# Chunk 0 of a Sinkhorn attention and feed-forward kernel: queries in both halves of the rows, sorted keys copied whole, and products of zeros in the head

## The chip, the cores and the metric

The kernel runs on one core of one Trainium2 chip. The metric is device time in microseconds (us) of one execution. A core has TensorE (PE: matrix products and transposes, results into PSUM), VectorE (DVE), ScalarE (ACT), GpSimd (POOL) and SyncE (SP), each with its own instruction queue that is worked off in order, and DMA engines that move data between the HBM and SBUF. The engines wait for each other by semaphores.

## The reference

Attention with sorted blocks, followed by a feed-forward stage. There are 4 batches of 8 heads, 768 positions of 64 elements, in 8 blocks of 96. A Sinkhorn loop turns each head's 8x8 matrix into a nearly doubly stochastic one; keys and values of a block become sums over all blocks with these weights; each block of queries then attends to its own sorted block.

```python
P = sort_net
for _ in range(5):
    P = np.exp(P - np.max(P, axis=-1, keepdims=True))
    P = P / (np.sum(P, axis=-1, keepdims=True) + 1e-09)
    P = P / (np.sum(P, axis=-2, keepdims=True) + 1e-09)
k_sorted = np.einsum('bhij,bhjcd->bhicd', P, k_b)
v_sorted = np.einsum('bhij,bhjcd->bhicd', P, v_b)
scores = scale * np.matmul(q_b, k_sorted.transpose(0, 1, 2, 4, 3))
attn = softmax(scores)
x = np.matmul(attn, v_sorted)        # (B*S, 512) after a transpose
h = x @ w_in                         # 512 -> 2048
out = (h * np.cos(h)) @ w_out        # 2048 -> 512
```

## The kernel before

The 3072 tokens go through in 8 chunks of 384: chunk n is four blocks (`IC` = 4) of one batch, all 8 heads. The order of instructions on each engine is the order of the program text (`tc.manual_schedule()`), so a helper that is called earlier stands earlier in every queue that it uses. Chunk n's feed-forward (`moe_up`, then `moe_down`) carries in its slots the attention of chunk n + 1. Chunk 0 has nothing to stand beside it: its attention is the head of the program.

The head runs so. The 8x8 matrices of two batches lie in one group of 128 rows, so there are two groups g. After a first normalization, four Sinkhorn rounds (the loop over `it`, lines 311 to 337) alternate between engines: ScalarE takes exponentials (line 313), TensorE sums columns by a product with the matrix `same` (`product`, line 252), VectorE takes reciprocals and forms the next matrix (lines 332 to 335). `spread` (line 273) writes a group's final weights into a block matrix `bds`. In rounds 1 and 2 `q_turn` (line 286) transposes the queries of chunk 0 on TensorE, sixteen pieces a call, and ScalarE copies them out of PSUM one round later.

With the weights, `v_turn` (line 405) lays out a second copy for the values. `k_sort_0` (line 349) makes the sorted keys of chunk 0: products of the loaded keys (`kbuf`) with the weights leave in PSUM, for each pair of positions, 64 rows for the even position and 64 for the odd one. Four calls cover 16, 16, 8 and 8 pairs, alternating between VectorE and ScalarE. Each call copies its tile to SBUF in four pieces of 64 rows, one for each half of the heads and each parity, so that a head's even and odd keys end in the same 64 rows of `kT[0]`. `v_sort_b` (line 416, called through `v_next`) makes the sorted values, eight columns a call, and copies them out on ScalarE; from the fifth call on it needs `vperm`, the values that GpSimd reorders (`v_permute`, line 167).

Then come four blocks u of 96 queries. `qk` (line 459) makes the scores of a block, eight products of 96 columns (`scores`, line 390), and VectorE takes the row maximum (line 454) and subtracts it (line 455). `expo` is the exponential on ScalarE (line 479). `p_transpose` turns the probabilities on TensorE (line 503), `av` multiplies with the values (line 516) and normalizes on VectorE (lines 523, 525), `x_transpose` turns the result (line 541) for `moe_up`. There, `up` (line 546) takes eight products per pair of 128 features (line 553), a cosine on ScalarE (line 557) and a product on VectorE (line 560). The first `moe_up(0, ...)` covers half of the chunk, the 192 tokens of blocks 0 and 1, and holds the rest of the attention of chunk 0 in its slots.

PSUM tiles come from two pools: `big` (three tiles of two banks) and `acc` (two tiles of one bank). A tile is reused when what read it is done. `keep_warm` (line 216) multiplies a tile of zeros with itself, 256 columns a time, into a `big` tile that nobody reads: 16 times at the start, and three times at each of three places of the Sinkhorn rounds.

Of the kernel before, what the change touches and what calls it, by code (L numbers as in the profile page):

```python
# [18 lines left out]
def kernel(  # L19
# [117 lines left out]
    def q_of(n, e):  # L137
        return q_turned[n % 2][:, e]
# [76 lines left out]

    def keep_warm(times):

        idle = big.tile([128, 256], FP32, name="idle", tag="big")
        for _ in range(times):
            nc.tensor.matmul(  # L220
                idle[:], warm[:], warm[:, :1].to_broadcast([128, 256]), start=True, stop=True)
# [40 lines left out]
    sk = [product(L[g], maskj) for g in range(NG)]  # L262
# [22 lines left out]

    def q_turn(n, z, pool, tag):
# [3 lines left out]
        ps = pool.tile([128, 2, IC, QR, blk // QR], BF16, name="qps", tag=tag)  # L290
# [11 lines left out]
        if n == 0:  # L302
            return [place(0, slice(0, 128))]
# [7 lines left out]
    for it in range(4):  # L311
        for g in range(NG):
            nc.scalar.activation(E[g][:], T[g][:], AF.Exp, scale=ci[g][:])
        if it > 1:
            copy_on(A, *turned[0])
        sk = [product(same, E[g]) for g in range(NG)]
        if it in (1, 2):
            turned = q_turn(0, it - 1, big, "big")
        keep_warm((3, 0, 0, 3)[it])
# [6 lines left out]
        elif it == 2:  # L326
# [11 lines left out]

    nc.vector.tensor_copy(
# [3 lines left out]
    MH = H2 * IC  # L343

# [4 lines left out]
    def k_sort_0(ih, t0, nt, eng, pool, tag):  # L349

        ps = pool.tile([128, nt, 2 * MH], FP32, name="ks", tag=tag)
# [10 lines left out]
    def k_sort_1(t0, eng, pool, tag):  # L362
        ps = pool.tile([128, 8, 2 * NB], FP32, name="ks", tag=tag)
# [5 lines left out]
    def k_sort_g(t0, eng, pool, tag):  # L369
        ps = pool.tile([128, 4, 4 * NB], FP32, name="ks", tag=tag)  # L370
# [19 lines left out]
    def scores(out, n, u, h2, hp):  # L390
        x = (u * H2 + h2) * blk
        if n == 0:
            rows = slice(hp * D, (hp + 1) * D)
            nc.tensor.matmul(
                out[:blk], q_of(0, 0)[rows, x:x + blk], keys_of(n, u, h2, hp)[rows],
                start=True, stop=True)
        else:

            nc.tensor.matmul(  # L399
                out, q_of(n, hp)[:, x:x + 128], keys_of(n, u, h2, hp), start=True, stop=True)  # L400
# [4 lines left out]
    def v_turn():  # L405
        ps = big.tile([128, 128], FP32, name="bdp", tag="big")
# [400 lines left out]
```

## Time and profile before

| | |
|---|---|
| three runs | 251.34, 249.9, 251.37 us; median 251.34 |
| profiled execution: span from first to last instruction | 248.0 us |
| median less that span | 3.3 us |
| mean granted TensorE clock over the span | 0.945 |
| busy: TensorE products | 231.1 us (93%) |
| busy: VectorE | 175.8 us (71%) |
| busy: ScalarE | 157.3 us (63%) |
| busy: GpSimd | 88.2 us (36%) |
| chain that ended last: TensorE | 75% of the span |
| chain that ended last: up products (line 553), down products (line 570) | 32%, 24% |

The profile is of one execution, taken with the hardware profiler. Its own time is not among the three runs; its span leaves out what lies ahead of the first and behind the last instruction. In lines of the timeline the columns are the start, the time from the first start to the last end of a group, the engine, the source line, what is written and read, and the count; a bracket gives the idle time of the engine ahead of it and what ended it. A product's time holds its latency, so neighbours overlap, and a busy TensorE need not stream at its full rate. "PEclk" is the share of the full clock that TensorE was granted.

### The profile page before, as it was taken

Reading aid. Unit: us, or ns where it says so; the run is one execution under the profiler, and the core shown is the slowest. Engines: PE = TensorE matmul, PEld = TensorE weight load, DVE = VectorE, ACT = ScalarE, POOL = GpSimd, SP = SyncE. Lnnn points to the kernel's source line nnn. Section 1 sums busy time; section 2 is a strip of 40 time slices with the busy share of each in tenths; the row PEclk is TensorE's granted clock in tenths of the full one; section 3 lists DMA queues with packets and bytes.
Section 4 is the critical chain, followed back from the end, with each engine's and each line's share of the span. In section 5 each row is a group of like instructions: output and inputs, shape, how many; then the busy total and the mean of one; then the engine's idle time right before and its main releaser. Section 6 shows DMA issues by size and latency. Waiting matters only on the chain.

```text
span 248.0 us, 5329 instructions
## 1 busy us (share of the span) xinstructions
PE 231.1 (93%) x2131; PEld 148.7 (60%) x2151; DVE 175.8 (71%) x322; ACT 157.3 (63%) x224; POOL 88.2 (36%) x104
## 2 busy tenths in 40 slices
PE   7887798878999999999999999999999999979994
PEld 5776696745566656665666556655565556435543
DVE  5579558897478876688568997898789759524710
ACT  4467846676568975789568866684667456634710
POOL 6369990799879707110353500800000000000000
PEclk9655569999999999999999999999999999999999
DMA  5999999895997058846897978937651650371012
GB/s 55 232 193 174 197 201 231 134 213 105 181 233 130 6 137 110 136 110 148 172 102 134 59 184 151 158 39 181 153 110 32 176 114 0 97 119 42 0 43 86
DMA packets 69001, 31.49 MB, mean 127 GB/s; under 512 B 57840, under 2 KB 64496, under 8 KB 68720
## 3 DMA queue, kind: packets, MB, share of 16 engines
q0 software_dynamic: 24048, 13.64, 40.8%
q1 hardware_dynamic: 43408, 15.28, 27.2%
q10 hardware_dynamic: 1520, 2.24, 2.8%
q8 instruction: 17, 0.28, 0.5%
q14 instruction: 8, 0.07, 0.1%
HBM read 27.27 MB, written 6.29 MB: 135 GB/s over the span
## 4 chain that ended last, share of the span: by engine, by line
PE 75%; DVE 10%; ACT 6%; DMA 5%; issue 2%; ACTq 0%; DVEq 0%; SPq 0%
PE h L553 32%; PE o L570 24%; PE sc L399 3%; PE av L516 3%; DMA vperm<-p_buf 2%; PE pps L503 2%; ACT p_buf L479 2%; DVE kTs L282 2%; PE ks L346 2%; PE vs L432 1%; DVE gg L560 1%; PE o L771 1%; DVE xn L525 1%; PE vs L422 1%; PE xps L541 1%
## 5 line engine op out<-in xcount | busy, mean ns | idle before, releaser
L553 PE MATMUL h<-xT,w_in_t 128*128 128x384 bf16 (+1 forms) x576 | 93.3, 313 | 2.1 <-DVE gg L560 0.8
L570 PE MATMUL o<-w_out_t,gg 128*128 128x512 bf16 x348 | 84.0, 379 | 1.6 <-DVE s L455 0.5
L557 ACT ACTIVATE c<-h,half_pi 128x768 f32<-128x768 f32 (+1 forms) x72 | 59.7, 830 | 36.2 <-PE h L553 33.9
L560 DVE TENSOR_TENSOR gg<-c,h 128x768 bf16<-128x768 f32 (+1 forms) x72 | 61.3, 859 | 25.2 <-ACT c L557 25.1
L553 PEld LDWEIGHTS <-w_in_t 128*128 128x128 bf16 x576 | 53.8, 100 | 29.7 <-issue 2.9
L570 PEld LDWEIGHTS <-gg 128*128 128x128 bf16 x368 | 33.6, 98 | 33.6 <-DVE s L455 0.7
L454 DVE TENSOR_REDUCE mx<-sc 96x4 f32<-96x384 f32 (+1 forms) x43 | 31.9, 741 | 3.2 <-PE sc L399 2.3
L455 DVE TENSOR_TENSOR s<-sc,mx 96x384 f32<-96x384 f32 (+1 forms) x43 | 32.2, 749 | 2.3
L177 POOL COPY vperm<-kv 64x1536 bf16<-64x1536 bf16 (+1 forms) x10 | 28.2, 2841 | 6.2 <-DMA kv<-in_v_dram 5.2
L479 ACT ACTIVATE p_buf<-s 96x768 bf16<-96x768 f32 x32 | 27.6, 894 | 2.4 <-ACT o_s L280 1.0
L280 ACT COPY o_s<-o 128x512 f32<-128x512 f32 (+1 forms) x18 | 10.3, 573 | 25.0 <-PE o L570 23.8
L525 DVE TENSOR_TENSOR xn<-av,r 96x512 bf16<-96x512 f32 x32 | 22.0, 686 | 1.1
L280 ACT CAST kTs<-ks 128x512 bf16<-128x512 f32 (+2 forms) x31 | 14.1, 456 | 6.2 <-PE ks L346 6.0
L134 POOL DMA_DIRECT2D kv<-in_q_dram x24 | 16.0, 675 | 3.1 <-DMA kv<-in_v_dram 2.2
L399 PE MATMUL sc<-kTs,q_turned 128*128 128x96 bf16 x224 | 16.1, 206 | 0.9 <-DVE s L455 0.7
L523 DVE RECIPROCAL r<-av 96x8 f32<-96x8 f32 x32 | 6.4, 199 | 14.7 <-PE av L516 14.6
L399 PEld LDWEIGHTS <-q_turned 128*128 128x128 bf16 x224 | 12.8, 98 | 4.8 <-DVE s L455 1.3
L282 DVE COPY o_s<-o 128x512 f32<-128x512 f32 (+1 forms) x7 | 4.5, 647 | 12.1 <-PE o L771 8.6
L557 ACT ACT_TABLE_LOAD x8 | 10.3, 1283 | 0.9 <-ACT o_s L280 0.7
L134 POOL DMA_DIRECT2D q_mem<-in_q_dram x16 | 10.6, 675 | 0.3 <-issue 0.3
L280 ACT CAST pair<-vs 96x512 bf16<-96x512 f32 (+1 forms) x12 | 8.7, 728 | 2.5 <-PE vs L432 2.0
L516 PEld LDWEIGHTS <-pT 96*128 96x128 bf16 (+1 forms) x160 | 7.8, 106 | 3.4 <-issue 1.2
(96 smaller groups left out, 212.8 us busy)
## 6 DMA issues: line engine op xcount, KB each, us to landing
out_dram<-o_s SPq DMA_DIRECT2D x15, 256.0 KB, 2.6
w_in_t<-in_moe_w_in_dram POOLq DMA_DIRECT2D x4, 512.0 KB, 10.6
w_out_t<-in_moe_w_out_dram POOLq DMA_DIRECT2D x4, 512.0 KB, 12.9
out_dram<-o_s ACTq DMA_DIRECT2D x8, 256.0 KB, 2.5
kv<-in_k_dram POOLq DMA_DIRECT2D x2, 768.0 KB, 13.3
kv<-in_v_dram POOLq DMA_DIRECT2D x2, 768.0 KB, 16.5
pair<-in_k_dram POOLq DMA_DIRECT2D x2, 768.0 KB, 11.5
kv<-in_v_dram POOLq DMA_DIRECT2D x6, 256.0 KB, 6.2
```

The source lines that it names most:

```text
L134: nc.gpsimd.dma_start(out=q_heads[:, i, :, e], in_=src[:, ih * IC + i, :, e])
L177: nc.gpsimd.tensor_copy(dst, src)
L280: eng.copy(dst, src)
L399: nc.tensor.matmul(out, q_of(n, hp)[:, x:x + 128], keys_of(n, u, h2, hp), start=True, stop=True)
L454: nc.vector.reduce_max(mx[:], scv, axis=AX.X)
L455: nc.vector.tensor_tensor(s_t[n, u][:, part[0]:part[0] + w], scv, mx.to_broadcast([blk, w, H2, blk]), op=ALU.subtract)
L479: nc.scalar.activation(dst, src, AF.Exp, scale=scale)
L525: nc.vector.tensor_tensor(xn.rearrange("p h e d -> p e h d"), avv[:, :, :, :D], r.to_broadcast([blk, 2, H2, D]), op=ALU.mult)
L553: nc.tensor.matmul(h[:, f2, :w], w_in_t[:, kk, f * 128:(f + 1) * 128], xT[n][:, kk, lo:hi], start=(kk == 0), stop=(kk == KC - 1))
L557: nc.scalar.activation(c[:, :, :w], h[:, :, :w], AF.Sin, bias=half_pi[:, 0:1])
L560: nc.vector.tensor_tensor(gt[n, fp][:, :, lo:hi], c[:, :, :w], h[:, :, :w], op=ALU.mult)
L570: nc.tensor.matmul(o[:], gt[n, f // 2][:, f % 2, ts * 128:(ts + 1) * 128], w_out_t[:, f, :], start=(f == 0), stop=(f == FC - 1))
```

## The change

Four things change in the head.

1. `q_turn` for chunk 0 gives way to `q_twice`: the queries of each half of the heads (`hp`) are transposed to rows 0 to 63 and again to rows 64 to 127. That makes 64 transposes in place of 32 and four copies on ScalarE (`q_place`) in place of two. Round 1 has sixteen transposes, round 2 thirty-two, round 3 sixteen. A pair of calls shares a PSUM tile. Two of the copies follow the Sinkhorn loop, one ahead of `v_turn` and one behind it.
2. `k_sort_0` for the first half copies its PSUM tile whole, one copy of 128 rows in place of four of 64. Even keys then stand in rows 0 to 63 and odd keys in rows 64 to 127 (`kdup`).
3. `scores_0` multiplies even and odd keys apart: per block, sixteen products of 48 columns in place of eight of 96, into two banks; maximum and subtraction read the two banks in an order that interleaves them (`p j x t`).
4. Products of zeros (256 columns each) are put in at many places: `fill` queues a number of them for the next PSUM tile, `fill_behind` writes them to the second bank of the tile allocated last. In all there are 73 such products in the program, against 25. PSUM tiles are now all allocated through `psum`, as flat tiles of a fixed size.

In round 2 the loads `load_w_in(3)`, `load_q(1)` and `load_w_out` are issued; they move to round 3.

```diff
+    def zeros_into(dst, times):
+        for _ in range(times):
+            nc.tensor.matmul(
+                dst, warm[:], warm[:, :1].to_broadcast([128, 256]), start=True, stop=True)
+
+    def fill(times):
+        pending[0] += times
+
+    def fill_behind(times):
+        zeros_into(last[0][:, 512:768], times)
+
+    def psum(pool, shape, name, tag, dtype=FP32):
+        flat = pool.tile([128, 1024 if tag == "big" else 512], FP32, name=name, tag=tag)
+        zeros_into(flat[:, :256], pending[0])
+        pending[0], last[0] = 0, flat
...
-    def product(lhs, rhs):
-        ps = acc.tile([128, nb], FP32, name="sk", tag="acc")
+    def product(lhs, rhs, zeros=0):
+        fill(zeros)
+        ps = psum(acc, [128, nb], "sk", "acc")
...
-    sk = [product(L[g], maskj) for g in range(NG)]
+    sk = [product(L[g], maskj, g) for g in range(NG)]
...
+    def q_twice(z, hp):
+        if hp == 0:
+            q_ps[z] = psum(big, [128, 2, 1024], "qps", "big", BF16)[:, :, :TC * 2].rearrange(
+                "d s (e i r p) -> d s e i r p", e=2, i=IC, r=QR)
+        ps = q_ps[z][:, hp]
+        for rows in (slice(0, D), slice(D, 2 * D)):
+            for e in range(2):
+                for r in range(QR):
+                    nc.tensor.transpose(
+                        ps[rows, e, :, r],
+                        q_rows[:, (z * 2 + e) * 2 + hp, r * D:(r + 1) * D], ident[:blk, :blk])
+
+    def q_place(z, hp, eng):
+        dst = q_of(0, hp)[:, :QW].rearrange("d (i h c) -> d h i c", h=H2, c=blk)
+        copy_on(eng, dst[:, z * 2:z * 2 + 2],
+                q_ps[z][:, hp].rearrange("d e i r p -> d e i (r p)"))
...
         if it > 1:
-            copy_on(A, *turned[0])
-        sk = [product(same, E[g]) for g in range(NG)]
-        if it in (1, 2):
-            turned = q_turn(0, it - 1, big, "big")
-        keep_warm((3, 0, 0, 3)[it])
+            q_place(0, it - 2, A)
+        sk = [product(same, E[g], g * (0, 2, 1, 1)[it]) for g in range(NG)]
+        for x in ((), (0,), (1, 2), (3,))[it]:
+            q_twice(x // 2, x % 2)
+        keep_warm(6) if it == 0 else None
...
-        elif it == 2:
+        elif it == 3:
             load_w_in(3)
...
+    fill(2)
+    q_place(1, 0, A)
...
+    kdup = kTs[:, 0, 2]
...
+        if ih == 0:
+            copy_on(eng, kdup[:, :, t0:t0 + nt], ps.rearrange("p t m -> p m t"))
+            return
...
+    def scores_0(sc, u):
+        for hp in range(2):
+            for h2 in range(H2):
+                j, x = hp * H2 + h2, (u * H2 + h2) * blk
+                w = 128 if x + 128 <= QW else blk
+                for t in range(2):
+                    rows = slice(t * D, (t + 1) * D)
+                    nc.tensor.matmul(
+                        sc[:w, t, j * HT:(j + 1) * HT], q_of(0, hp)[rows, x:x + w],
+                        kdup[rows, hp * MH + h2 * IC + u], start=True, stop=True)
...
+        if n == 0:
+            scores_0(sc, u)
+            scv = sc[:blk, :, :H * HT].rearrange("p x (j t) -> p j x t", t=HT)
+            mx = small.tile([blk, H], FP32, name="mx", tag="mx")
+            nc.vector.reduce_max(mx[:], scv, axis=AX.XY)
...
     v_turn()
+    q_place(1, 1, A)
     k_sort_0(0, 0, 16, V, *B)
     k_sort_0(0, 16, 16, A, *C)
     k_sort_0(0, 32, 8, V, *B)
     k_sort_0(0, 40, 8, A, *C)
+    fill(4)
     v_next(A, *B)
+    fill_behind(5)
     v_next(A, *B)
+    fill_behind(4)
     qk(0, 0)
...
     expo(0, 0, True)
     v_next()
+    fill(7)
     p_transpose(0, 0, A, *B)
...
+    fill(5)
     p_transpose(0, 1, A, *B)
+    fill(3)
     av(0, 0, True)
+    fill(3)
     av(0, 1, True)
     expo(0, 2, True)
     expo(0, 3, True)
+    fill(3)
     x_transpose(0, 0, V, *C)
+    fill(3)
     x_transpose(0, 1, V, *C)
+    fill(4)
```

More of the change, by code (lines that the diff above doesn't have):

```diff
@@ L546, in up @@
     def up(n, fp, lo=0, hi=TC):
-        h = big.tile([128, 2, 512], FP32, name="h", tag="big")
+        h = psum(big, [128, 2, 512], "h", "big")
         w = hi - lo
@@ L566, in down @@
         if half == 0:
-            out_ps[ts] = acc.tile([128, Dm], FP32, name="o", tag="acc")
+            out_ps[ts] = psum(acc, [128, Dm], "o", "acc")
         o = out_ps[ts]
```

51 lines of the change are left out of this document (26 added, 25 removed).

## The prediction

> **What bounds the kernel now.** I read first the page: span, the row of TensorE and that of its granted clock (40 slices of 6.2 us).
>
> ```profile
> span 248.0 us, 5329 instructions
> ...
> PE   7887798878999999999999999999999999979994
> ...
> PEclk9655569999999999999999999999999999999999
> ```
>
> From slice 7 on TensorE is busy nine tenths at the full clock, so what the head saves moves the end forward one for one. In slices 2 to 6 the clock is about one half. A table by microsecond dates its fall to 7.8 (0.89 is 0.22 us at one half) and its return to 35.1:
>
> ```profile
> core 0: us, PE busy (x) PEld busy (x) DVE busy (x) ACT busy (x) POOL busy (x), PEclk, DMA share, GB/s
> ...
> 7.00:8.00 1.00, 0.39 (x2) 0.30 (x2) 0.57 (x6) 0.54 (x2) 0.47 (x2) 0.89 0.93 197
> ...
> 35.00:36.00 1.00, 1.00 (x24) 0.97 (x23) 0.84 (x3) 0.59 (x3) 1.00 (x1) 0.95 1.24 205
> ```
>
> The timeline of the head (start, time, engine, line, count) shows what half a clock costs and who waits:
>
> ```profile
> 1.04 3.53 PE L220 MATMUL idle<-warm 128*128 128x256 bf16 x16 [1.04 <-DVE warm L209]
> 6.49 0.49 PE L220 MATMUL idle<-warm 128*128 128x256 bf16 x3
> ...
> 14.39 2.60 ACT L280 CAST kTs<-ks 64x256 bf16<-64x256 f32 x8 [0.70 <-PE ks L346]
> 14.39 2.95 DVE L282 CAST kTs<-ks 64x256 bf16<-64x256 f32 x8
> ...
> 17.49 0.56 PE L394 MATMUL sc<-kTs,q_turned 64*96 64x96 bf16 x8 [0.39 <-DVE kTs L282]
> 18.08 0.95 DVE L454 TENSOR_REDUCE mx<-sc 96x8 f32<-96x768 f32 x1 [0.74 <-PE sc L394]
> 19.07 0.95 DVE L455 TENSOR_TENSOR s<-sc,mx 96x768 f32<-96x768 f32 x1
> ...
> 20.98 1.06 ACT L479 ACTIVATE p_buf<-s 96x768 bf16<-96x768 f32 x1
> ...
> 29.20 1.44 PE L553 MATMUL h<-xT,w_in_t 128*128 128x192 bf16 x8 [0.45 <-DVE xT L282]
> 30.67 0.58 ACT L557 ACTIVATE c<-h,half_pi 128x384 f32<-128x384 f32 x1 [0.97 <-PE h L553]
> 32.59 0.58 ACT L557 ACTIVATE c<-h,half_pi 128x384 f32<-128x384 f32 x1 [1.34 <-PE h L553]
> 34.51 0.58 ACT L557 ACTIVATE c<-h,half_pi 128x384 f32<-128x384 f32 x1 [1.34 <-PE h L553]
> ```
>
> A zero product takes 3.53/16 = 0.22 us in the first row and (0.49 - 0.27)/2 = 0.11 in the second (0.27 is one product's latency): the clock came up about 4.4, whatever the page's first digit says. The first scores (17.49) wait for VectorE's key copies, and up to 26 VectorE is nearly full: four pairs of 0.95. From 29.2 the period of 1.92 (30.67, 32.59, 34.51) is TensorE's at half clock: eight up products 1.28 (1.44 less the last one's latency) and eight transposes 0.64.
>
> **What holds the clock.** Busy rows do not tell: between 4.4 and 7.8 TensorE was 2.66 of 3.40 us busy, and the clock fell; between 48.7 and 52.1 it was 2.07, and the clock stayed. So I count streaming, that is products by their spacing. 4.4 to 7.8: six zeros at 0.11, 0.2 of the time, fell. 28.3 to 31.7: up products, transposes, 2.8 us or 0.82, no rise. 31.7 to 35.1: 3.2 us or 0.94, rose. 48.7 to 52.1: sixteen up products at 0.08, eight scores, 0.47, held. Holding needs something between 0.2 and 0.47, rising between 0.82 and 0.94. The stretches of 3.4 us are a yardstick: the clock fell 3.4 us after the dense zeros ended.
>
> The Trainium skill, "TensorE: Matmul & The Clock Gate", section "Why this matters for your kernels", says a drop needs a TensorE gap of over about 3 us. This trace disagrees: before the fall the longest gap was 0.51 us; by that rule the changed kernel could never fall.
>
> **The change, part by part**, if the clock holds from 4.4 on.
>
> 1. Sinkhorn rounds. Sixteen transposes take 0.56 instead of 0.86 (40.61 against 10.47), a product pair 0.39 instead of 0.59. But round 2's first sixteen transposes write the PSUM tile of round 1's and wait until ScalarE has copied those out (0.78, here 9.9 to 10.7); sixteen more follow, 32 in 0.90 (row at 69.89), and round 3's column sums stand behind them in TensorE's queue: 11.6 against 11.27. The other zeros (two, one, one) run while the exponential of the second group is awaited. Weights for the first group come at 12.85 instead of 12.66: +0.2.
>
> 2. Key copies. Whole tiles of 128x512 take 0.68 on VectorE and 0.59 on ScalarE (rows at 59.95 and 57.55); the half tiles I put between half of that and the 64-partition rows, 0.42 and 0.37. VectorE starts as before (its second group sets that) and is done at 15.5, not 17.34. ScalarE has two query copies more, 1.56, and is done at 15.55 instead of 16.99.
>
> 3. Zeros ahead of the scores. The built program shows that the first four wait for VectorE's first key copy (15.1); the five and the four "behind" write the tile that ScalarE is copying out and so wait for that copy. TensorE works in order: 15.1 + 0.43 (four zeros) + 0.45 (value products) + 0.64 (copy and two hand-overs) + 0.54 (five zeros) + 0.45 + 0.69 + 0.43 (four zeros) = 18.75, where the scores start, against 17.49: +1.3. What the copies gave is spent, and more.
>
> 4. Scores to h. Sixteen products of 48 columns stream as much as eight of 96, in both halves of the array's rows at once, as the eight do: nothing. VectorE's reading of two banks at 96x768 is not in the trace; the same count in one order took 0.95; 0.95 it stays, 1.05 at most (+0.8 over four pairs). VectorE is the bound: with 0.65 to its first row and 1.87 a pair its fourth pair ends at 18.75 + 0.65 + 7.55 = 26.95 (25.9 before). The seven and five zeros before the probabilities' transposes run while exponentials are awaited; were those earlier, they would cost 0.75 and 0.54. The transposes at 0.56 instead of 0.87 are hidden behind ScalarE's value copies (24.64, 1.04). Behind that pair VectorE has two reciprocals (0.20) and two normalizations (0.69), then come four transposes (0.34), a copy (0.36) and 0.1 of hand-over: 26.95 + 2.6, h at 29.55 against 29.20: +0.35. The zeros of this part (three, three, three, three, four) run in front of what waits for VectorE; only the three that wait for ScalarE's second copy of probabilities delay the second values' products, by 0.33, and VectorE is later than that.
>
> 5. First up pass. Eight products take 0.82 instead of 1.44, so the first cosine starts at 30.4 instead of 30.67. The period falls from 1.92 to 1.05: VectorE's 0.56 + 0.55, TensorE 0.66 + 0.34. Third cosine: 30.4 + 2.1 = 32.5 instead of 34.51: -2.0; a quarter of a us more in the next values' products. Behind 35.1 both run alike: -2.3.
>
> What could eat that later: weights and keys have landed (the first output product at 51.96 waits for VectorE, not for a DMA); GpSimd's 11.2 us of value copies still wait for their load at 46.9, end at 58.1 and are needed at 70. load_w_in(3) and the loads behind it are issued in a later round, but in the same place of GpSimd's queue, behind 5.48 us of copies that end at 20.1: nothing.
>
> Sum against the profiled execution: span 248.0 - 2.3 = 245.7. Its span lies 3.3 under the median of 251.34; times lie at 249.9 to 251.37, so I put the 3.3 around it: 249.0. I take 248.9, as step 4 carries hand-overs that may overlap.
>
> **Rivals.**
>
> A short loss. The poorest stretches then are 4.4 to 7.8 (ten zeros, 0.33) and 7.8 to 11.2 (three zeros, thirty transposes at 0.026, 0.3, of which products only 0.1). If 0.3 is too little, the clock falls at 7.8 or 11.2. Back at 18: thirteen zeros and sixteen value products at half clock add about 1.0 and 0.4, the scores start 1.4 later, step 5 stays: 250.3. For it: 0.3 is nearer 0.2 than 0.47. Against: at half clock 14.6 to 18 streams only 0.66, and 0.82 did not raise it. The Trainium skill, same page, section "Part 4: PE-mode transpose", says that transposes do not count as busy; by it the clock falls at 11.2. No row here isolates transposes at the full clock; half of what this rival has of chance is for that cause.
>
> A long loss, the other side. At half clock the zeros are on the path with 0.21 each. Scores: three queues of sixteen transposes more before the weights (+1.75), thirteen zeros 2.8, value products 0.95 each, two copies: 22.7, so +5.2. h at 22.7 + 10.8 + 1.0 = 34.5. If the clock is back then, the third cosine is at 37.4 instead of 34.51: +2.8, 254.1. It decides if the clock, once lost, is not back by about 25; back at 35 costs 1.7 more, 255.8.
>
> That the zeros do nothing for the clock is the long loss; that they are not needed for it would show as a clock that holds with far fewer, and their price in step 3 as a loss without return.
>
> **How the numbers follow.** Clock held 0.50: if the bound lies anywhere between 0.2 and 0.47 on a scale of ratios, 0.3 is about half way. Short loss 0.20, long loss 0.30, since 0.66 falls short of what raised it before. A measurement tells about 1%, 2.5 us, from no change: faster is under 248.8, slower over 253.9. The held case lies at the first bound, 247.6 to 250 (0.8 above for the scores' reading and 0.3 for the sum; below it step 3, where five zeros and two hand-overs, 0.9, may partly run beside the copies, and 0.4 of what lies around the span): 0.32 faster, 0.18 same. Short loss 0.03 faster, 0.15 same, 0.02 slower; long loss 0.04 same, 0.26 slower. Faster 0.35, same 0.37, slower 0.28. The range leaves out the longest losses, 0.15, and the fastest of the held, 0.05: 247.6 to 254.6; the held case alone, 247.6 to 250.
>
> **What would show it.** A clock of 1.00 from 4.4 through 35; VectorE's two key copies near 0.68 and 0.42; ScalarE's first two value copies more than a us apart with the zeros between them; scores near 18.8; cosines a us apart from 30.4. A clock of 0.50 anywhere in between is a rival; scores before 17.5 would make step 3 wrong.

## The result and the profile after

| | before | changed |
|---|---|---|
| median | 250.68 us (249.16 to 252.68, 20 executions) | 255.01 us (251.66 to 261.35, 20 executions) |
| profiled execution, time and span | 249.9 and 248.0 us | 259.15 and 257.4 us |

The ratio is 1.0104, interval 1.0075 to 1.0134: slower by about 1%, clear of the noise, where the prediction has 248.9 and a range up to 254.6. The ratios of all comparisons here leave out executions over 1.5% above the fastest of their kernel; of the changed kernel these are nine of twenty, the profiled one among them, and its trace shows no disturbance but something that the change does.

The first two lines of the page of the changed kernel, and its row of TensorE:

```profile
span 257.4 us, 5562 instructions
...
PE   8965899888899999999999999997999999997995
```

TensorE's row shows 8 and 9 all through the head, which looks better than before's 7s and 8s, and says nothing of the clock at which it is busy. This page has no row of the granted clock, since nothing was recorded of it. The zeros tell it: sixteen took 3.60 us at the start, 0.22 each, four at 31.6 still stand 0.21 apart, and five at 34.5 took 0.73, a spacing of 0.11. The value products between them go from 0.05 to 0.03 apart at 34.3. So in this execution the clock stood at one half from the start to about 34.3. The timeline of the same execution:

```profile
1.04 3.60 PE L220 MATMUL idle<-warm 128*128 128x256 bf16 x16 [1.04 <-DVE warm L209]
...
15.05 5.54 POOL L177 COPY vperm<-kv 64x1536 bf16<-64x1536 bf16 x2 [4.91 <-DMA kv<-in_v_dram]
15.60 2.38 DVE L296 SCALAR_TENSOR_TENSOR bd<-maskp,ci,T 128x128 bf16<-128x128 f32 x1
...
17.91 2.79 DVE L382 COPY order<-ident 96x96 bf16<-96x96 bf16 x1
...
20.61 1.01 DVE L304 CAST kTs<-ks 128x512 bf16<-128x512 f32 x2
...
21.34 1.01 PE L220 MATMUL vs<-warm 128*128 128x256 bf16 x4 [4.10 <-DVE kTs L304]
...
23.88 1.22 PE L220 MATMUL vs<-warm 128*128 128x256 bf16 x5 [0.67 <-ACT vS L302]
...
26.63 1.01 PE L220 MATMUL vs<-warm 128*128 128x256 bf16 x4 [0.68 <-ACT vS L302]
...
27.57 0.50 PE L450 MATMUL sc<-kTs,q_turned 64*128 64x48 bf16 x16
...
34.50 0.73 PE L220 MATMUL pps<-warm 128*128 128x256 bf16 x5
...
39.34 0.82 PE L615 MATMUL h<-xT,w_in_t 128*128 128x192 bf16 x8
```

The scores start at 27.57, not 17.49 as before, and h at 39.34 instead of 29.20: all of the 10.1 us is lost ahead of the scores, and the 11.8 between them are unchanged. Two rows of VectorE are out of proportion. The second group's spread of weights (L296) takes 2.38 us and the copy of `order` (L382) 2.79. In the profile before, those two and GpSimd's copies stand so:

```profile
13.98 0.35 DVE L274 SCALAR_TENSOR_TENSOR bd<-maskp,ci,T 128x128 bf16<-128x128 f32 x1
14.25 0.23 DVE L339 COPY order<-ident 96x96 bf16<-96x96 bf16 x1
...
14.64 5.48 POOL L177 COPY vperm<-kv 64x1536 bf16<-64x1536 bf16 x2 [4.69 <-DMA kv<-in_v_dram]
```

Before, VectorE was through 0.16 us ahead of GpSimd. Now it starts behind it, and its two instructions end with GpSimd's two copies (about 17.9 and 20.6). VectorE works in order, so the key copies stand behind, and TensorE waits 4.10 us for them.

### The profile page after: what moved, and what is told of

Its sections match the earlier page's. It is cut to its first block, busy times and chain, and to the rows that moved or that the text cites. A ratio compares the mean times of both kernels' runs of the same rounds, so it can differ in the third digit from the quotient of the medians.

```text
span 257.4 us, 5562 instructions
## 1 busy us (share of the span) xinstructions
PE 238.5 (93%) x2263; PEld 153.6 (60%) x2263; DVE 178.9 (70%) x316; ACT 157.4 (61%) x220; POOL 88.3 (34%) x104
## 3 DMA queue, kind: packets, MB, share of 16 engines
q1 hardware_dynamic: 43408, 15.28, 26.4%
## 4 chain that ended last, share of the span: by engine, by line
PE 77%; DVE 9%; ACT 6%; DMA 5%; issue 2%; DVEq 0%; ACTq 0%
PE h L615 30%; PE o L632 24%; PE sc L439 3%; DMA vperm<-p_buf 3%; PE av L578 3%; PE vs L474 2%; PE idle L220 2%; PE ks L390 2%; PE vs L484 1%; PE o L844 1%; PE vs L220 1%; PE pps L565 1%; PE sk L276 1%; DVE gg L622 1%; DVE s L517 1%
## 5 line engine op out<-in xcount | busy, mean ns | idle before, releaser
L615 PE MATMUL h<-xT,w_in_t 128*128 128x384 bf16 (+1 forms) x576 | 91.4, 308 | 3.2 <-DVE o_s L304 1.6
L632 PE MATMUL o<-w_out_t,gg 128*128 128x512 bf16 x368 | 87.2, 379 | 0.5 <-DVE s L517 0.5
L615 PEld LDWEIGHTS <-w_in_t 128*128 128x128 bf16 x576 | 52.4, 98 | 30.6 <-issue 2.7
L517 DVE TENSOR_TENSOR s<-sc,mx 96x384 f32<-96x384 f32 (+1 forms) x39 | 28.4, 728 | 2.5 <-DVE mx L516 0.5
L516 DVE TENSOR_REDUCE mx<-sc 96x4 f32<-96x384 f32 (+1 forms) x39 | 28.1, 721 | 2.3 <-PE sc L439 2.3
L302 ACT CAST kTs<-ks 128x512 bf16<-128x512 f32 (+2 forms) x25 | 12.5, 504 | 5.2 <-PE ks L390 5.1
L302 ACT CAST vS<-vs 96x512 bf16<-96x512 f32 x16 | 9.1, 581 | 10.5 <-PE vs L474 10.5
L220 PEld LDWEIGHTS <-warm 128*128 128x128 bf16 x73 | 9.3, 138 | 9.2 <-issue 5.7
```

The lines of the kernel that those rows point to most:

```text
L302: eng.copy(dst, src)
L516: nc.vector.reduce_max(mx[:], scv, axis=AX.X)
L517: nc.vector.tensor_tensor(s_t[n, u][:, part[0]:part[0] + w], scv, mx.to_broadcast([blk, w, H2, blk]), op=ALU.subtract)
L615: nc.tensor.matmul(h[:, f2, :w], w_in_t[:, kk, f * 128:(f + 1) * 128], xT[n][:, kk, lo:hi], start=(kk == 0), stop=(kk == KC - 1))
L632: nc.tensor.matmul(o[:], gt[n, f // 2][:, f % 2, ts * 128:(ts + 1) * 128], w_out_t[:, f, :], start=(f == 0), stop=(f == FC - 1))
```

## The experiments

The times are medians, and each ratio is to runs of the kernel before on the same chip. The expectations name the theories by letters. C: the time is decided by the clock alone. P: two of VectorE's instructions meet GpSimd's copies at a shared port of SBUF. S: the thirteen zeros ahead of the scores cost their time in series. H: those thirteen hold the clock. L: the zeros behind the scores alone bring the gain. K: the doubled queries and whole key copies are needed for it. U: the clock counts a product by the share of the array that it fills. T: only streaming time counts. F: TensorE's packets of instructions delay DMA transposes. D: those transposes are late because the head is early.

To say where time goes, I take how much later (+) or earlier (-) than in the profile before a kernel reaches the same product of VectorE in the feed-forward stage, in us:

| at about | 38 | 101 | 164 | 178 | 235 |
|---|---|---|---|---|---|
| changed, first profile | +7.5 | +7.5 | +7.5 | +9.6 | +9.4 |
| changed, second profile (1) | +0.9 | +0.8 | +0.8 | +2.8 | +1.7 |
| without the thirteen, port free (6) | -2.3 | -2.1 | -2.1 | +1.4 | +0.3 |
| before with late zeros, port free (12) | -2.9 | +1.6 | +2.9 | +2.9 | +3.3 |
| the same, zeros 512 wide (13) | -1.9 | -0.3 | +0.9 | +1.4 | +0.9 |
| before with 28 small products (14) | -0.1 | +3.1 | +4.5 | +4.5 | +4.2 |
| 13 with seven zeros cut small (17) | -1.1 | -0.8 | -0.8 | +1.1 | +0.4 |

**1. The changed kernel once more.** No edit.

> The changed kernel once more, nothing edited, for a second profile. Theory P (port): VectorE's spread of the second group's weights and its copy of order stand behind GpSimd's two value copies, whatever the clock: if those two start later than GpSimd's first copy, they end with GpSimd's first and second copy, and TensorE idles 3 to 5 us ahead of the first values' product. Theory C (clock alone): where the clock comes up at 4.4 the two stay at 0.35 and 0.23 us, and only the clock tells this profile from the last. Time 251.5 to 259 by both.

Measured: 254.24 (252.63 and 255.84). In this execution (span 250.9) the clock came up. The clock's row on its page:

```profile
PEclk9985899999999999999999999999999999999999
```

And its timeline:

```profile
14.02 0.35 DVE L296 SCALAR_TENSOR_TENSOR bd<-maskp,ci,T 128x128 bf16<-128x128 f32 x1
14.29 0.23 DVE L382 COPY order<-ident 96x96 bf16<-96x96 bf16 x1
...
14.44 1.01 DVE L304 CAST kTs<-ks 128x512 bf16<-128x512 f32 x2
...
14.85 5.44 POOL L177 COPY vperm<-kv 64x1536 bf16<-64x1536 bf16 x2 [4.82 <-DMA kv<-in_v_dram]
15.17 0.60 PE L220 MATMUL vs<-warm 128*128 128x256 bf16 x4 [0.52 <-DVE kTs L304]
...
17.31 1.22 PE L220 MATMUL vs<-warm 128*128 128x256 bf16 x5 [0.68 <-ACT vS L302]
...
20.06 1.01 PE L220 MATMUL vs<-warm 128*128 128x256 bf16 x4 [0.68 <-ACT vS L302]
...
21.00 0.50 PE L450 MATMUL sc<-kTs,q_turned 64*128 64x48 bf16 x16
...
32.73 0.82 PE L615 MATMUL h<-xT,w_in_t 128*128 128x192 bf16 x8
33.75 0.83 PE L615 MATMUL h<-xT,w_in_t 128*128 128x192 bf16 x8
34.77 0.83 PE L615 MATMUL h<-xT,w_in_t 128*128 128x192 bf16 x8
```

VectorE's two instructions are through before GpSimd starts, and its key copies are done at 15.45 (17.34 before). Yet the scores start 5.55 us behind them, at 21.00; before it was 0.15. The five zeros take 1.22, so the clock is at half again. A table by stretches of the clock (the columns as in the prediction; PEclk follows the busy times):

```profile
9.50:12.90 3.40, 2.97 (x59) 2.62 (x57) 1.76 (x13) 2.24 (x6) 0.52 (x1) 1.00 0.94 199
12.90:16.30 3.40, 2.88 (x63) 2.40 (x61) 2.04 (x9) 2.39 (x5) 1.46 (x1) 1.00 1.10 193
16.30:19.70 3.40, 2.41 (x17) 1.75 (x17) 0.00 (x0) 0.87 (x2) 3.40 (x2) 0.50 1.24 206
```

The clock was up from 6.08 to 16.32, fell with TensorE busy 2.88 of 3.40 us, and came back at 26.56. So no case of the prediction happened as it stood: the clock did not hold, it was lost in another place than the rivals had it, and it came back past the 25 that the long loss names.

**2, 3. The port.** In 2 the copy of `order` moves into the first Sinkhorn round and the second group's spread behind the last transposes of the head:

```diff
-            if it == 3:
+            if it == 3 and g == 0:
                 spread(g)
+        if it == 0:
+            nc.vector.tensor_copy(order...)
...
     x_transpose(0, 1, V, *C)
+    spread(1)
```

> The changed kernel with two VectorE steps moved out of GpSimd's value copies: order is copied in round 0 of the normalization, the second group's weights are spread behind the second transposed output. Theory P: the key copies on VectorE start as soon as the key products are there, the 4.1 us of TensorE's wait go, and the time falls by 2.5 to 4 us against the changed kernel, to 249 to 252. Theory C: the wait is only a place where a slow clock's time is counted; under 1 us of difference, 253 to 255.

In 3 the kernel before is given the collision: its `order` copy goes behind the first key copy.

```diff
     k_sort_0(0, 0, 16, V, *B)
+    nc.vector.tensor_copy(order...)
```

> The kernel before, with the copy of order put behind VectorE's first four key copies, so that it comes up while GpSimd copies values. Theory P: that copy of 0.23 us ends when GpSimd's first copy ends, near 17.4, VectorE's other key copies end at 19 instead of 17.3 and the time grows by 1 to 1.7 us. Theory C: the copy takes 0.23 us wherever it stands; no difference.

Measured for 2: 255.37, five of six at 252.70 to 256.49; 1.0145, interval 1.0084 to 1.0207. The sixth, the profiled one, took 469.15 at half clock to its end, and only its head can be read: the key copies follow their products at once (15.80) and the scores start at 22.82 at half clock, instead of 27.57. The median misses what P forecast, 249 to 252. That fits the second profile, where the two instructions escaped GpSimd and there was no wait to win; the two executions of 2 with a mean clock of 0.99 or more took 256.1 and 256.5, and those of the changed kernel 259.5 in the median. Measured for 3: 251.98; 1.0066, interval 1.0041 to 1.0090. Its timeline:

```profile
14.73 5.48 POOL L177 COPY vperm<-kv 64x1536 bf16<-64x1536 bf16 x2 [4.92 <-DMA kv<-in_v_dram]
15.85 1.74 DVE L607 COPY order<-ident 96x96 bf16<-96x96 bf16 x1
17.60 1.22 DVE L282 CAST kTs<-ks 64x128 bf16<-64x128 f32 x4
```

The same copy that takes 0.23 us alone takes 1.74 here, to the end of GpSimd's first copy, and the median is 1.7 higher. In its profile 0.7 of that is there at 38 us, and 1.0 comes between 101 and 164, where the program is that of before; that part was not followed up. So the collision is shown in both directions: 3 puts it in, and 2 takes the wait out of the head. The Trainium skill, "SBUF — State Buffer", section "Who interferes with whom", says it: a VectorE instruction with two inputs in SBUF contends with a GpSimd instruction that reads SBUF, and between one in a two-port mode and GpSimd the one that comes first keeps the shared ports for its whole instruction while the other is blocked. The trace agrees: 0.35 became 2.38 (two inputs) and 0.23 became 2.79 (a copy), while the key copies, which read PSUM, took 1.01 for two beside GpSimd in the second profile. That the copy of `order` ran in a two-port mode is concluded, not recorded.

**4 to 7. The zeros in series.** 5 is the changed kernel without the thirteen; 4 keeps 24 zeros, sixteen at the start and eight up to the end of the Sinkhorn loop, and none behind it; 6 and 7 are 5 and 4 with the edit of 2. The edit of 5 is the first part of that of 4, whose core is:

```diff
     k_sort_0(0, 40, 8, A, *C)
-    fill(4)
     v_next(A, *B)
-    fill_behind(5)
     v_next(A, *B)
-    fill_behind(4)
     qk(0, 0)
...
-    fill(7)
     p_transpose(0, 0, A, *B)
...
-    fill(5)
     p_transpose(0, 1, A, *B)
-    fill(3)
     av(0, 0, True)
...
-        sk = [product(same, E[g], g * (0, 2, 1, 1)[it]) for g in range(NG)]
+        sk = [product(same, E[g]) for g in range(NG)]
```

> The changed kernel with 24 products of zeros instead of 73 (16 at the start, 3 and 3 in the first rounds, 2 ahead of the transposed weights). Theory P: VectorE is at its copy of order at 14.2 to 14.5, as before, so it goes through ahead of GpSimd or is caught; caught costs 2.7 us. Without thirteen zeros on the path, the scores start at 16 to 17 if it goes through, and the time is 248 to 250; caught, 251 to 252. Theory C with zeros that hold the clock: without them the clock falls at 7.8 and is back at 35, as before; 250 to 252, and the fastest times of the changed kernel (251.7) stay out of reach of its own median (255) for want of a clock, so no gain of more than 1 us over the kernel before.

> The changed kernel without the thirteen products of zeros ahead of the scores (four before the first value products, five and four behind ScalarE's copies); the other 60 stay. Theory S (serial zeros): in the second profile of the changed kernel these thirteen, run with half a clock, and their two waits of 0.68 us for ScalarE's copies put the scores at 21.0; without them the first scores start at 16.5 to 17.3, h at 28 to 29, and the time falls by 3.5 to 4.5 us, to 249.5 to 251.5 in the median. Rival H (these zeros hold the clock for what follows): without them the clock comes back later than 26.6, by one or two of its steps of 3.4 us, and at most 2 us are won, 252.5 or more.

> The same without the thirteen zeros, and with the copy of order in round 0 and the second group's weights spread behind the second transposed output, so that no VectorE step ahead of the scores meets GpSimd's value copies. Theory P (port): the slow end of the times goes (the changed kernel has 256 to 261 in nine of twenty), as key copies no longer wait up to 4 us where the clock stays low; median 249 to 250.5, highest under 254. Theory C (clock alone): median and highest as without this edit.

> The changed kernel with 24 products of zeros instead of 73 and with VectorE's two steps out of the way of GpSimd. Theory P: the 2.8 us that the copy of order took in the run with 24 zeros go; scores near 17.3 to 17.8, time 251.5 to 252.2, so the turned queries and whole key copies by themselves are worth nothing or cost up to 1 us. Rival: the wait only hid the first value products behind it; gain under 1.5 us, 253 or more.

| | median (range, executions) | ratio, interval | clock up, down, up | scores | h |
|---|---|---|---|---|---|
| 4 | 254.55 (254.26 to 255.18, 4) | 1.0167, 1.0113 to 1.0221 | 4.86, 8.27, 35.57 | 19.2 | 31.19 |
| 5 | 251.51 (248.23 to 255.54, 10) | 0.9952, 0.9907 to 0.9997 | 4.18, 11.0, 28.07 | 17.38 | 31.06 |
| 6 | 251.04 (248.46 to 252.12, 12) | 0.9988, 0.9952 to 1.0024 | 5.95, 12.78, 26.43 | 16.32 | 29.51 |
| 7 | 252.25 (250.28 to 254.27, 10) | 1.0024, 0.9991 to 1.0058 | 4.25, 7.66, 34.97 | 17.70 | 29.70 |

S holds: without the thirteen the median falls by 3.5 and the scores come 3.6 earlier than in the second profile; h gains only 1.7, to 31.06, where 28 to 29 was expected. H falls by its time (252.5 or more was its forecast): the clock is lost with the thirteen and lost without them, there at 11.0, before TensorE gets to where they stood, and it comes back at 28.07 against 26.56. 4 lies above what both theories gave; in its profile the copy of `order` was caught and took 2.82. P holds: from 4 to 7 the port gives 2.3, and from 5 to 6 the highest times drop from 255.5 to 252.1, though 6's median stays above its forecast (249 to 250.5). In spite of its ratio 5 has no gain over before by the medians of all executions (251.51 against 251.13). 7 shows the doubled queries and whole key copies by themselves: h at 29.70, no gain. The difference between 6 and 7 is the clock's return, 26.43 against 34.97, and that is what the 36 zeros bring that 6 has and 7 lacks, 28 of them behind the scores.

The port also explains a part of the spread. A mean granted clock of 0.99 or more has room for one stretch of 3.41 us at half clock on record at most. In all five profiles of such executions (the changed kernel's first, 2, 13, 14 and 15) the clock did not come up ahead of 27 us. I take it, untraced, to be so in the others. The changed kernel's five such executions have a median of 259.5 us, the other fifteen 254.0, a distance of 5.5. Without the thirteen zeros (5) the distance is 3.9, without the collision (2, leaving out the 469.15) 3.5, and without both (6) 1.5, between 251.3 in four and 249.8 in eight; but these are two to five executions each. The kernel before has 251.3 in 46 and 250.6 in 69. So the change made the kernel depend on whether the clock comes up at the start, and port and zeros both have a share in it.

**8. More zeros at the start.** An edit of 6:

```diff
-    keep_warm(16)
+    keep_warm(24)
```

> The run without the thirteen zeros and without the port's waits, with 24 products of zeros at the start instead of 16. If the spread of times comes from whether the clock's stretch of 3.4 us falls within the first zeros, 24 of them (5.1 us at half clock) make every start rise: times within 1.5 us of each other. They delay the first sums by 0.9 to 1.7 us. Median 249.5 to 251.5; if the clock holds no more surely, 251 to 253 with the same spread.

Measured: 250.51 (249.33 to 252.55, 10); 0.9992, interval 0.9956 to 1.0028. None of the ten has a clock of 0.99 or more, where 6 had four of twelve, which speaks for a safer start; ten executions do not prove it. But the clock still fell at 13.03, came back only at 30.10, and scores (18.19) and h (31.42) start 1.9 later than in 6. The spread, expected at 1.5, was 3.2.

**9, 10, 12. The late zeros alone.** 9 is the kernel before, with its own queries, keys and scores, and 28 zeros of the changed kernel:

```diff
+    fill(7)
     p_transpose(0, 0, A, *B)
...
+    fill(5)
     p_transpose(0, 1, A, *B)
+    fill(3)
     av(0, 0, True)
+    fill(3)
     av(0, 1, True)
...
+    fill(3)
     x_transpose(0, 0, V, *C)
+    fill(3)
     x_transpose(0, 1, V, *C)
+    fill(4)
```

> The kernel before (its queries, key copies and scores) with only the late products of zeros: seven and five ahead of the probabilities' transposes, three ahead of each of two values' products and two transposed outputs, four ahead of the first up products; 28 in all. Theory L (late zeros alone bring the gain): they stand where TensorE waits for VectorE and ScalarE anyway, the clock comes back at 25 to 29 instead of 35, the up products' period falls from 1.92 to 1.03, and the time falls by 2 to 2.6 us, to 248 to 249. Rival K (the keys and queries are needed for it): under 1 us.

12 is 9 with the edit of 2. 10 has that edit too, and the changed kernel's zeros up to the end of the Sinkhorn loop:

```diff
+    sk = [product(L[g], maskj, g) for g in range(NG)]
...
+        sk = [product(same, E[g], g * (0, 2, 1, 1)[it]) for g in range(NG)]
...
+        keep_warm(6) if it == 0 else None
...
+    fill(2)
```

> The same with the zeros in the normalization too (one and three more beside the first sums, six in round 0, two, one and one in the later rounds, two ahead of the transposed weights) and VectorE's copy of order and second spread out of the way of GpSimd. Theory L: where the clock comes up at the start it holds to 9 or 13 and the weights are ready 0.5 to 1 us earlier; where it does not, the zeros cost up to 1 us. Time 247.5 to 249.5, wider than the last. Rival: the early zeros cost more than they bring, over 249.5.

> The kernel before with the 28 late zeros, and with VectorE's copy of order and second spread out of the way of GpSimd. Theory P says that the kernel before is caught by the port in few executions only (its copy of order starts 0.4 us ahead of GpSimd's): 0 to 0.4 us faster than without this edit, 247.7 to 249.

Measured: 9 253.79 (251.13 to 254.27, 7), 1.0094, interval 1.0059 to 1.0129; 10 251.25 (249.90 to 252.36, 12), 1.0002, interval 0.9978 to 1.0026; 12 253.05 (252.61 to 254.04, 6), 1.0085, interval 1.0057 to 1.0113. K falls: 10, without them, comes out as 6 does (251.04), and at 38 us it is 2.7 ahead. For the head L is right: the clock is back at 24.8 in 12, h starts at 28.99, and at 38 us it is 2.9 ahead. For the end L is wrong: by 101 us it is 1.6 behind, and in the end 3.3. 10 misses its forecast (247.5 to 249.5) in the same way: it is 0.9 ahead at 101 and 1.2 behind at 235. What lies between is the same program as before. Something other than the head was changed.

**11. What the clock counts.** 6, with every zero behind the first sixteen on 64 rows of the array instead of 128; the time that it streams is the same.

```diff
     keep_warm(16)
+    rows = 64
```

> The run without the thirteen zeros and without the port's waits, with every product of zeros after the first sixteen on 64 of the 128 rows: same columns, same streaming time, half of the array. Theory U (a product counts by the share of the array it fills; over eight profiles every stretch of 3.4 us at or above 0.33 of the array's full-clock throughput held, every one at or below 0.31 fell, and those that rose had 0.36 or more): the stretch from 6 to 9.4 has 0.25 instead of 0.39 and falls, the one from 23 to 26.4 has 0.27 instead of 0.39 and does not rise; back at 33 to 36, time 251.5 to 253. Rival T (only the streaming time counts): clock and time as with full rows, back at 26 to 30, 250 to 251.

The clock's row on the page of 6:

```profile
PEclk9955899999999999999999999999799999999999
```

The same row of 11:

```profile
PEclk9655559999999999999999999999999999999999
```

Measured: 259.88 (256.39 to 260.65, 4), 1.0306, interval 1.0244 to 1.0367, far above what either theory gave; three of the four have no fall on record. In the trace the clock came up at 4.62, fell at 8.03 and was back at 38.8 only, although products streamed 0.84 to 0.98 of the time in four stretches between 21.7 and 35.3. Counted by the share of the array, these stretches come to 0.24 to 0.26. T falls, and U stands for the clock, though not for the time. Over the 17 profiles with a clock on record, I weighted every product of the first 60 us by columns, rows/128 and array columns/128 at the full clock. Of 143 stretches of 3.41 us at full clock that held, all had 0.38 or more but one (0.33); the 14 that fell had 0.31 or less but one (0.38). Of the stretches at half clock the 31 that rose had 0.36 or more but two (0.34), and none of the 72 others exceeded 0.36. Left out of the 72 are 22 stretches of 13, 14 and 15 ahead of the first change on record there; they have 0.36 or less but one, 0.38, at the very start of 13. By streaming alone the groups overlap widely: some fell with 0.64, some held with 0.38. It is a fit, and between 0.31 and 0.38 it does not decide. Only the rows were tested by a run of their own; that the columns of the array count in the same way rests on the fit.

**13. The late zeros in fewer instructions.** 12 with zeros of 512 columns, half as many: TensorE has 6 instructions more than in the kernel before instead of 56.

```diff
-    keep_warm(16)
+    keep_warm(8)
...
-    fill(7)
+    fill(3)
     p_transpose(0, 0, A, *B)
```

> The kernel before with late zeros and out of the port's way, as in the last but with zeros of 512 and 384 columns instead of 256, so that TensorE has 6 instructions more than the kernel before instead of 56. Theory F (fetch): TensorE's instructions come in blocks of 16 KB, one for each 256 of them, by the DMA engines; in thirteen profiles a DMA transpose of probabilities or outputs with such a packet in its flight took 4.1 to 5.7 us to land, and 2.6 without one, and 56 instructions more put a packet on the transposes at 90 and 120 us (waits of 1.8 and 1.9 us and a fallen clock). With the packets back in the places of the kernel before, the 2.9 us won by 37 us reach the end: 247.6 to 249. Rival D (transposes land late because the head is early against the loads, whatever the packets do): 252.5 to 253.5 again.

Measured: 250.92 (249.53 to 251.35, 12), 0.9987, interval 0.9959 to 1.0015: 2.1 better than 12 with the same work, and 2 short of what F gave. In its profile the clock came up at 27.4 only, so its lead at 38 us is smaller than 12's.

**14. Instructions without work.** The kernel before with 28 zero products of 32 columns where TensorE waits 1.2 us anyway, ahead of `p_transpose(0, 0)`. As in the changed kernel, all PSUM tiles are allocated through `psum`, which also writes the zeros; no run has that alone.

```diff
+        zeros_into(flat[:, :32], small_[0])
...
     v_next()
+    small_[0] = 28
     p_transpose(0, 0, A, *B)
```

> The kernel before with 28 products of zeros of 32 columns (56 instructions, 0.8 us) where TensorE waits 1.2 us for the first probabilities. Theory F: nothing changes in the head, the packets move 28 products forward, a packet falls on the transposes at 91 and 121 us, and 3 to 5 us are lost behind 85 us: 253.5 to 256. Rival D: the head keeps its times, so 250.5 to 252.

Measured: 253.30 (251.01 to 255.48, 12), 1.0079, interval 1.0049 to 1.0109. At 38 us it is level with before (-0.1), at 101 it is 3.1 behind. TensorE's timeline in the profile before:

```profile
92.32 0.94 PE L516 MATMUL av<-vS,pT 96*128 96x65 bf16 x16
...
93.32 1.89 PE L570 MATMUL o<-w_out_t,gg 128*128 128x512 bf16 x8
```

The same products in the timeline of 14:

```profile
92.17 0.42 PE L572 MATMUL av<-vS,pT 96*128 96x65 bf16 x8
...
94.45 0.43 PE L572 MATMUL av<-vS,pT 96*128 96x65 bf16 x8 [1.86 <-DMA pT<-p_buf]
```

Sixteen value products ran in one go; now the second eight wait 1.86 us for a DMA transpose of probabilities. Its landing times, in the answer on that tile between 84 and 97 us, in the profile before:

```profile
DMA to landing us min/median/max: 2.6/2.6/2.7
```

The same answer for 14:

```profile
DMA to landing us min/median/max: 2.6/3.0/4.4
```

And what follows, in the table by stretches of 14:

```profile
95.50:99.00 3.50, 3.50 (x25) 1.94 (x23) 0.85 (x3) 0.23 (x1) 3.50 (x6) 0.51 0.70 44
```

Behind the wait the clock falls to 0.51 for a whole stretch, in which half of 3.4 us, 1.7, can be lost. What is in the way is in the answer on DMA queues of 14 between 91 and 94 us; before has no such packet there, its own comes at 94.2:

```profile
q8 instruction: 1, 0.02, 1.8%
```

These packets hold instructions, 16 KB at a time, 17 or 18 packets an execution. They are TensorE's by the count: the page of the changed kernel has 4526 instructions of TensorE (products and weight loads) and at most 316 of any other engine, about 266 for each of 17 packets, an estimate. Over 18 profiles the DMA transposes beside which such a packet began, at least 0.5 us behind their issue and ahead of their landing (103), landed in 4.15 us in the median, the others (581) in 2.63. The Trainium skill, "Runtime: NRT & Kernel Launch", section "Instruction fetch mechanics", describes fetches in blocks of 16 KiB and 256 instructions and calls the cost of crossing one mostly hidden. On the size the trace agrees. The cost measured here is another one: in 14 TensorE waits for transposes that land late beside the fetch, and 28 idle products made the kernel 2.4 us slower. D falls, since the head of 14 is not early.

**15 to 17. Moving the packets.** 15 is 6 and 16 is the changed kernel, with four and two of the seven zeros ahead of `p_transpose(0, 0)` cut into 32 and 16 products of 32 columns; 17 is 13 with seven wide zeros cut into 112 of 32 columns. The edits of 16 and 17:

```diff
-    fill(7)
+    fill(5)
+    small_[0] = 16
     p_transpose(0, 0, A, *B)
```

```diff
-    fill(3)
+    cut[0] = 48
     p_transpose(0, 0, A, *B)
...
-    fill(3)
+    cut[0] = 48
     p_transpose(0, 1, A, *B)
-    fill(1)
+    cut[0] = 16
     av(0, 0, True)
```

> The run without the thirteen zeros and out of the port's way, with four of the seven zeros of 256 columns ahead of the first probabilities' transposes cut into 32 of 32 columns: the same columns, 254 instructions more than the kernel before instead of 198, two short of a whole block. Theory F: the packet at 168 us, whose transposes cost 2.0 us and a stretch of half clock (1.7), moves away; 1.5 to 3.5 us faster than without, 247.5 to 249.5. Rival D: as without, 250.5 to 251.5.

> The changed kernel with two of the seven zeros ahead of the first probabilities' transposes cut into 16 of 32 columns: 252 instructions more than the kernel before instead of 224. Theory F: the packet on the transposes at 171 us moves away, 1 to 2 us faster than the changed kernel (255.0 in its 20 executions), 253 to 254. Rival D: no difference over 0.5.

> The kernel before with wide late zeros and out of the port's way, where seven of the late zeros of 512 columns are cut into 112 of 32: the same columns, 216 instructions more than the kernel before, so that the packets of instructions come 40 instructions later than in it (as in the run with 24 first zeros, whose lead at 37 us reached the end but for 0.1 us). Theory F: the lead of 2 to 2.9 us at 37 us is kept but for 0 to 1.5 us, 248 to 249.7. Against it stand the two shifts that missed: if places can't be set by counting, 250.5 to 252.

Measured: 15 251.28 (248.79 to 251.51, 12), 1.0000, interval 0.9974 to 1.0026; 16 255.07 (252.99 to 260.20, 6), 1.0121, interval 1.0072 to 1.0170; 17 250.24 (249.21 to 251.88, 12), 0.9975, interval 0.9949 to 1.0002. 15 and 16 made no difference, so F's forecasts for them missed and those of D came true. 17 lies above F's forecast too. It does the same work as 12 and 13 and is 2.8 and 0.7 faster: at 101 us it is still 0.8 ahead, where 12 had lost 4.5. So with the same work the times differ by microseconds, and by 14 and the landing times I put that down to where the packets fall; but counting instructions did not place them well enough to aim: they are fetched ahead by an amount that I could not tell within 2 us. By its median over all executions no version is more than 0.8 us faster than the kernel before.

## Why the prediction was wrong

**The clock, the step that failed.** "If the clock holds from 4.4 on" had a chance of 0.50 and happened in no profile of the changed kernel or of its variants: in the second profile the clock fell at 16.32 and stood at one half to 26.56. The step behind it took every product at its spacing and set the bound for holding between 0.2 and 0.47. By that count the stretch that fell has 0.40, more than the 0.3 that the prediction called the poorest, and one in 6 fell with 0.64, far above the bound. Query transposes (96 rows, 64 columns), key and value products and scores (64 rows) fill half of the array or less, and were counted by their time alone. Counted by share of the array, the stretches from 9.5 to 16.3 of the second profile come to 0.33 and 0.26, and the second ends in the fall. The prediction also took 4.4 for the rise from one execution; it came at 4.1 to 6.2 in fourteen profiles, and not ahead of 27 us in the first of the changed kernel and in 2, 13, 14 and 15.

**VectorE "starts as before"** (step 2) is right only where the clock came up. At half clock the weights are late, the port adds 4.1 us of TensorE's wait, and no rival had it.

**Step 3 mis-sized.** The order was right: four zeros behind VectorE's first copy (15.17, forecast 15.1), then two groups that each follow a ScalarE copy by 0.68. But at half clock a zero is 0.21 to 0.22, so the scores start at 21.00 and not 18.75. Without the thirteen they start at 17.38 and the median is 3.5 lower (5).

**Step 4 mis-sized.** Reading two banks took 0.95, as forecast, but from scores to h it had 10.8 and it took 11.73 (11.71 before). Most of the difference lies behind VectorE's fourth pair: VectorE waits 0.56 for the first value products there, a wait that the step left out although before has one of 0.48, and h starts 3.36 behind that pair instead of 2.6.

**Right.** Steps 1 and 2 in the second profile: weights at 12.71 (forecast 12.85), VectorE's key copies done at 15.45 (15.5). Step 5: a period of 1.02 (1.05), and from h to the end of the first up pass 2.6 are gained (2.65, from +0.35 to -2.3).

**"What could eat that later: nothing"** missed the instruction packets. In the second profile the lag goes from +0.8 to +2.8 at 178 us, where value products wait 1.31 and 0.63 us for DMA transposes; a packet is in flight there. So the second profile stands at +3.5 at h, +0.9 behind the up pass and +2.8 at 178. At 235 us it is at +1.7, and its span is 2.9 longer; the last 1.2 were not followed up.

**The base.** A time lies 1.7 to 1.9 over its span in the 115 executions of the kernel before that have both on record, so the 3.3 was wrong: it held the distance of the profiled execution from the median too. By that distance the profiled execution is the one of 249.9, so its time is among the three runs after all. With 1.8, the sum would have been 247.5.

**The rivals.** The long loss gave 254.1 to 255.8 and the median is 255.0, so the prediction's second choice came near the time, but partly by luck, through terms that cancel: its scores at 22.7 lie between 21.00 and 27.57, and it lacked port and packets. The short loss had the clock back at 18; it was 26.6.

## What to carry to other kernels

Zeros that are to hold the clock belong where TensorE waits for something that does not wait for them; thirteen in a row with the scores cost 3.5 us of the median, while those behind the scores brought the head forward. Before an instruction of VectorE that reads two operands from SBUF, or copies within it, look what GpSimd will be doing if everything ahead runs at half clock: an escape by 0.16 us is no escape. After a change of the number of TensorE's instructions, read the DMA transposes far behind the change before judging the change by its time.

## What was not expected of the hardware

The clock is decided in stretches of 3.41 us: between changes on record inside a span lie 6.83, 10.24, 17.07 and 27.30 us, which are 2, 3, 5 and 8 of them. What counts, by the fit, is how much of the array is filled: in experiment 11 zeros on half of the rows, streaming 0.84 to 0.98 of the time, did not raise it, while the full-row zeros of 6 did at 26.4. It fell with TensorE busy 2.88 of 3.40 us, so a long gap is not needed for a fall. The Trainium skill, "TensorE: Matmul & The Clock Gate", section "Why this matters for your kernels", which the prediction weighed, warns of gaps of over about 3 us and does not say that nothing else lets the clock drop. Transposes count for something here: the stretch from 9.5 to 12.9 of the second profile held, though its other products come to 0.12 of the array, and eight stretches without transposes fell with 0.21 or more. How much one counts was isolated by no run. DMA transposes land later where a packet of TensorE's instructions is fetched beside them: 4.15 us against 2.63.
